# Half of a quad's block moves issued from GpSimd's queue in a fused attention and MLP kernel

## The chip, the cores and the metric

The kernel runs on one core of a Trainium2 chip. A core has five engines with a queue of instructions each: TensorE (PE in the profile), VectorE (DVE), ScalarE (ACT), GpSimd (POOL) and SyncE (SP, which only issues DMAs). Instructions of one engine run in order; between engines, semaphores order them. DMAs are issued from SyncE, ScalarE or GpSimd and are carried out by 16 DMA engines that all of them share. The metric is the device time of one execution in microseconds (us). Before the change it was 395.21 us, the median of two runs (394.13 to 396.29).

## What is computed

Attention with a squared ReLU in place of the softmax, for 8 batches and 12 heads of 448 positions with 64 dimensions, and then a two-layer MLP over all 3584 positions with a PReLU between the layers:

```python
scores = scale * np.matmul(q, k.transpose(0, 1, 3, 2))      # scale = 1/8
attn = np.maximum(scores, 0.0) ** 2 / S                     # S = 448
attn_out = np.matmul(attn, v)
x = attn_out.transpose(0, 2, 1, 3).reshape(B * S, H * D)    # 3584 x 768
h = x @ w_in                                                # 768 x 2048
g = np.maximum(h, 0.0) + alpha * np.minimum(h, 0.0)
out = g @ w_out                                             # 2048 x 768
```

Inputs and output are float32 in HBM. The kernel computes in bfloat16 and accumulates in float32.

## The kernel before

**Quads.** The attention is done in 24 quads, numbered n = 0 to 23: a quad is four heads of one batch, three quads make a batch. A position is written as 7·p + j, with p on 64 partitions and j = 0..6; a *chunk* (n, j) holds the scores of all four heads for the keys of one j.

**From HBM to T.** `load_qk` (L112 to L124) loads a quad's q and k from GpSimd's queue, which casts them to bfloat16 on the way, into the `raw` tiles (three buffers each). The score matmuls contract over the 64 dimensions, so q and k have to lie with the dimension on the partitions: tile `T`, four buffers. For quads 0 to 4, `turn_pe` transposes on TensorE. For quads 5 to 23, `turn_dma` (L194) does it in two steps. DVE transposes each 32x32 block where it lies (L202, one instruction for q and one for k, into a `perm` tile, or into space of `w_mix` that is not yet in use for quads 5, 7 and 8). Then eight plain DMAs (L208) move whole 32-partition stripes between partition groups, SBUF to SBUF, 56 KB each: for each half m (partitions 64m to 64m+63, which hold two of the four heads), for each source stripe a and each destination stripe b. They are issued in the order m, a, b.

**Scores.** `score_mm` (L215) makes a chunk's scores from T in a pair of PSUM banks: for r = 0 it reads partitions 0 to 63 of T, which is the half m = 0, and for r = 1 partitions 64 to 127, the half m = 1. From quad 5 on a chunk is eight matmuls of line L229, four for each r. `relu` (L237 on ScalarE, L239 on DVE) and `square` (L248, L250) follow; `attnv` (L253) multiplies by v once all seven chunks of a quad are there and writes `xT`, the MLP's input.

**MLP.** `f1_mm` (L294) makes one 128-wide block of h in a PSUM bank with six matmuls; `f1_out` takes the negative part on ScalarE (`neg`, L300, two buffers) and joins it on DVE into `gT` (L301). The second layer is L319 for some tiles, and L354 for pairs of tiles that go through a Strassen-like scheme with sums of `gT` (L350) and of the weights (`w_mix`, L332).

**Order of the work.** There is no scheduler. A plan is written out as strings of short words (L525 to L537), and `Walk.step` emits the instructions of a word in that order on all engines. The words that matter here: `cAAD` emits chunks, with the engine of each ReLU; `s0D` a square; `v` an attention-times-v; `f` one block of the first layer; `h`, `e` and `E` parts of one; `d6D` is `turn_dma` of quad 6; `Lq`, `Lv`, `Li` and `Lo` are loads of q and k, v, w_in and w_out. From quad 11 on, a word `n` calls `prepare(n)` (L427), which does `turn_dma(n)`, then loads q and k of quad n + 2 and v of quad n + 1. The first part of the plan around quads 5 to 9 reads (L526, L527, cut):

```python
... m o f s0D f cAAA s0D s1D d5D f f s0D f l5 Lq6 f Lq7 Lq8 g00 Lo1,0,4 s0D cADA s2D vDA cDD ...
B h h cAA h s0D s0D h v d6D l6 Lo1,4 Lv6 h E E E d7D f E f E f f d8D f l8 cAAA s1D f Lq9 f Lv7 ...
```

**Buffers set the waits.** PSUM has eight banks. `take_pair` and `one` (L81, L96) hand out the bank, or pair of banks, that was taken longest ago, so a matmul into a bank waits for whatever still reads it. A load of q waits until the transposes of the quad three before have read its buffer; a load of v (five buffers) until the attention-times-v of five quads before. Each queue also has eight DMA semaphores that it uses in turn, so a DMA waits until the one eight before it on that queue has landed.

**Queues.** Before the change, GpSimd's queue carries only loads (and a few small things at the start), SyncE's the block moves of L208 and the stores of the output (L310).

Of the kernel before, what the change touches and what calls it, by code (L numbers as in the profile page):

```python
# [21 lines left out]
def kernel(  # L22
# [10 lines left out]
    nc = tc.nc  # L33
# [160 lines left out]
    def turn_dma(n, eng="A"):  # L194
        if n in (5, 7, 8):
            w = w_mix[2 + n % 2].rearrange("p k c -> p (k c)")[:, :4 * NJ * D]
            x = w.rearrange("p (i b f c) -> p i b f c", i=2, b=2, c=32)
        else:
            x = perm_pool.tile([128, 2, 2, 2 * NJ, 32], BF16, tag="perm", name="perm")
        for i, name in enumerate("qk"):  # L200
            rows = raw.pop((n, name)).rearrange("p w j d -> p (w j) d")
            nc.vector.transpose(x[:, i].rearrange("p b f c -> p f b c"), rows.rearrange("p f (b c) -> p f b c", b=2))  # L202
        t = T_pool.tile([128, 2, NJ, 128], BF16, tag="T", name="T")
        z = t.rearrange("p i j c -> p i (j c)").rearrange("p i (a f c) -> p i a f c", a=2, c=32)
        for m in range(2):
            for a in range(2):
                for b in range(2):
                    nc.sync.dma_start(out=z[64 * m + 32 * b:64 * m + 32 * b + 32, :, a],  # L208
                                                      in_=x[64 * m + 32 * a:64 * m + 32 * a + 32, :, b])
        T[n] = z  # L210

# [215 lines left out]
    def prepare(n, eng="A"):  # L427
        if n < NQ:
            turn_dma(n, eng)
            land(n)  # L430
        if n + 2 < NQ:
            load_qk(n + 2)
        if n + 1 < NQ:
            load_v(n + 1)
# [4 lines left out]
    class Walk:  # L439
# [12 lines left out]
        def step(self, w):  # L452
# [41 lines left out]
            elif c == "w":  # L494
                i, half = int(rest[0]), int(rest[1])
                weight_mix(i, 4 * half, 4 * half + 4)
            elif c == "g":
                f2(self.b // 2, int(rest[0]), int(rest[1]))
            elif c == "n":
                prepare(self.quad, rest or "A")  # L500
                self.quad += 1
            elif c == "x":
                cast0(int(rest[0]), int(rest[1]), rest[2])
            elif c == "t":
                turn_pe(int(rest[0]), ((rest[1], int(rest[2]), int(rest[3]), rest[4]),))
            elif c == "d":
                turn_dma(int(rest[:-1]), rest[-1])
            elif c == "l":
                land(int(rest))
            elif c == "L":  # L510
                n = [int(x) for x in rest[1:].split(",")]
                {"q": load_qk, "v": load_v, "i": load_w_in, "o": load_w_out}[rest[0]](*n)
            elif c == "i":
                warm(int(rest))
            elif c == "y":
                bank = min(range(8), key=lambda i: (taken[i], i))
                for _ in range(int(rest)):
                    nc.tensor.matmul(psum[:, bank, :128], idle, idle, start=True, stop=True)
            elif c == "z":
                two_queues.append(1)  # L520
            elif c == "b":
                nc.vector.tensor_scalar(beta_sb, alpha_sb, -1.0, 1.0, ALU.mult, ALU.add)
# [48 lines left out]
```

## Time and profile before

| | |
|---|---|
| median of two runs | 395.21 us |
| the profiled execution's own time | 394.87 us |
| its span, first to last instruction | 393.1 us |
| mean granted TensorE clock | 0.991 |
| block moves L208 on SyncE | 152 (128 from `perm`, 24 from `w_mix`), 56 KB each |
| one issue of L208 on SyncE, median | 0.596 us |
| issue to landing of L208, min / median / max | 2.0 / 3.9 / 6.6 us |
| q and k loads of L123 on GpSimd | 76, median issue 0.60 us |
| waits of GpSimd's q loads for DVE's transposes | 129.8 us, 13 times |

The profile is of one execution, and its times count from the first instruction. Busy time is that of compute instructions on an engine; a DMA issue stands in the trace with the time that the queue took to issue it, and its landing is known from the semaphore that it raises. "A <- B" names B as what ended A's wait. In a timeline, a line is start, duration, engine, source line, operation, tiles and count, with the idle time before it in brackets; a line of many matmuls is a run of them. In a table by stages, a line is a stretch of time with the busy time and the count of each engine in it. Matmuls are pipelined, so the pitch from one to the next is the time that counts, not the duration of one.

### The profile page before, as it was taken

How to read it: one execution, taken by the hardware profiler on the slowest of the kernel's cores; microseconds unless marked ns; L12 is line 12 of the kernel's file. 1: busy time of each engine (PE TensorE's matmuls, PEld its weight loads, DVE VectorE, ACT ScalarE, POOL GpSimd, SP SyncE). 2: the span in 40 equal slices, each digit the busy share in tenths (PEclk: the TensorE clock that was granted, in tenths of full speed). 3: DMA queues.
4: the chain of work that ended last, by engine and by line, in shares of the span. 5: the costliest groups of instructions: out<-in, count | busy, mean ns of one | idle time of the engine just before them, and what ended most of it. 6: DMA issues, size and time to landing. Idle time of an engine off the chain costs nothing.

```text
span 393.1 us, 9204 instructions
## 1 busy us (share of the span) xinstructions
PE 372.5 (95%) x3633; PEld 195.9 (50%) x3637; DVE 304.9 (78%) x467; ACT 258.8 (66%) x384; POOL 86.4 (22%) x140
## 2 busy tenths in 40 slices
PE   8899999499989998999989999899999999999996
PEld 6454555144444454545545455445555555555563
DVE  4988988655996989867788886888969875865753
ACT  5987674456766656768668676786587785874400
POOL 8566563500330323011220311303000000000000
PEclk9999999889999999999999999999999999999999
DMA  9999999952677755726766257664333321220024
GB/s 148 191 203 202 207 209 206 223 109 47 100 147 152 117 95 79 166 42 116 136 109 140 43 97 141 108 144 66 76 62 81 76 49 26 64 65 9 2 51 110
DMA packets 51676, 43.38 MB, mean 110 GB/s; under 512 B 8753, under 2 KB 51121, under 8 KB 51633
## 3 DMA queue, kind: packets, MB, share of 16 engines
q0 software_dynamic: 27744, 22.59, 40.0%
q1 hardware_dynamic: 23216, 19.62, 19.6%
q8 instruction: 28, 0.46, 0.5%
q10 hardware_dynamic: 672, 0.59, 0.4%
q14 instruction: 16, 0.12, 0.1%
HBM read 45.62 MB, written 11.01 MB: 144 GB/s over the span
## 4 chain that ended last, share of the span: by engine, by line
PE 72%; DVE 12%; SPq 6%; DMA 4%; issue 3%; ACT 1%; DVEq 0%; ACTq 0%
PE psum L294 30%; PE psum L354 24%; PE psum L260 7%; PE psum L229 6%; SPq L208 5%; DVE perm L202 3%; DVE at L250 3%; DMA T<-perm 2%; PE psum L319 2%; DVE gT L301 2%; DMA T<-w_mix 1%; DVE S L350 1%; PE psum L171 1%; DVE rl L239 1%; PE psum L221 1%
## 5 line engine op out<-in xcount | busy, mean ns | idle before, releaser
L294 PE MATMUL psum<-xT,w_in_sb 128*128 128x448 bf16 x768 | 152.6, 356 | 0.4 <-DVE gT L301 0.4
L237 ACT ACTIVATE rl<-psum 128x896 bf16<-128x896 f32 x128 | 111.4, 929 | 25.9 <-PE psum L229 23.4
L301 DVE SCALAR_TENSOR_TENSOR gT<-neg,beta_sb,psum 128x448 bf16<-128x448 f32 x128 | 84.0, 675 | 36.1 <-ACT neg L300 34.9
L294 PEld LDWEIGHTS <-w_in_sb 128*128 128x128 bf16 x768 | 74.2, 99 | 75.0 <-issue 9.7
L300 ACT ACTIVATE neg<-psum 128x448 f32<-128x448 f32 x128 | 68.9, 546 | 55.3 <-PE psum L294 39.6
L250 DVE TENSOR_TENSOR at<-rl 128x896 bf16<-128x896 bf16 x105 | 62.1, 617 | 3.8 <-ACT rl L237 3.7
L248 ACT ACTIVATE at<-rl 128x896 bf16<-128x896 bf16 x63 | 58.3, 951 | 1.5 <-DVE rl L239 1.2
L123 POOL DMA_DIRECT2D qraw<-in_q_dram x38 | 22.6, 600 | 137.3 <-DVE perm L202 129.8
L354 PEld LDWEIGHTS <-S 128*128 128x128 bf16 x384 | 36.4, 98 | 32.7 <-issue 10.0
L239 DVE TENSOR_SCALAR rl<-psum 128x896 bf16<-128x896 f32 x40 | 43.2, 1086 | 9.3 <-PE psum L229 8.1
L354 PE MATMUL psum<-w_mix,S 128*128 128x384 bf16 x288 | 49.9, 326 | 0.0
L229 PE MATMUL psum<-T 64*32 64x448 bf16 x1064 | 38.0, 358 | 7.1 <-DMA T<-perm 5.4
L354 PEld LDWEIGHTS <-gT 128*128 128x128 bf16 x296 | 28.3, 98 | 20.2 <-issue 1.8
L260 PE MATMUL psum<-at,vraw 64*64 64x448 bf16 x672 | 36.6, 352 | 0.0
L354 PE MATMUL psum<-w_out_sb,gT 128*128 128x384 bf16 x192 | 34.0, 326 | 0.0
L130 POOL DMA_DIRECT2D vraw<-in_v_dram x24 | 17.7, 739 | 51.7 <-PE psum L260 49.7
L229 PEld LDWEIGHTS <-T 64*32 64x32 bf16 x1064 | 12.7, 90 | 29.3 <-issue 26.9
L260 PEld LDWEIGHTS <-vraw 64*64 64x64 bf16 x672 | 19.4, 106 | 14.7 <-issue 6.5
L359 DVE TENSOR_TENSOR osb<-psum,u 128x384 f32<-128x384 f32 (+2 forms) x37 | 19.7, 542 | 9.0 <-PE psum L354 8.4
L123 POOL DMA_DIRECT2D kraw<-in_k_dram x38 | 22.9, 614 | 3.3 <-DMA vraw<-in_v_dram 1.4
L319 PE MATMUL psum<-w_out_sb,gT 128*128 128x256 bf16 (+1 forms) x124 | 22.5, 325 | 0.9 <-DVE gT L301 0.5
L274 DVE TENSOR_SCALAR xT<-psum 128x448 bf16<-128x448 f32 x24 | 14.9, 623 | 10.0 <-PE psum L260 9.9
(46 smaller groups left out, 240.2 us busy)
## 6 DMA issues: line engine op xcount, KB each, us to landing
out_dram<-osb SPq DMA_DIRECT2D x91, 96.0 KB, 2.2
T<-perm SPq DMA_DIRECT2D x128, 56.0 KB, 3.6
vraw<-in_v_dram POOLq DMA_DIRECT2D x24, 224.0 KB, 6.1
qraw<-in_q_dram POOLq DMA_DIRECT2D x38, 112.0 KB, 3.3
kraw<-in_k_dram POOLq DMA_DIRECT2D x38, 112.0 KB, 4.7
w_in_sb<-in_moe_w_in_dram POOLq DMA_DIRECT2D x16, 192.0 KB, 8.2
w_out_sb<-in_moe_w_out_dram POOLq DMA_DIRECT2D x4, 512.0 KB, 10.4
T<-w_mix SPq DMA_DIRECT2D x24, 56.0 KB, 5.3
```

The lines of the kernel that those rows point to most:

```text
L123: nc.gpsimd.dma_start(out=t[64 * m:64 * m + 64].rearrange("p w j d -> p w (j d)"), in_=flat[2 * g + m])
L229: nc.tensor.matmul(ps[lo:lo + 32, r, :S], t[64 * r:64 * r + 64, 1, a, NJ * c + j], moving, start=True, stop=True)
L237: nc.scalar.activation(rl, ps[:, :, :S], ACTF.Relu)
L239: nc.vector.tensor_scalar(rl, ps[:, :, :S], 0.0, None, ALU.max)
L248: nc.scalar.activation(a, rl, ACTF.Square)
L250: nc.vector.tensor_tensor(a, rl, rl, ALU.mult)
L260: nc.tensor.matmul(ps[64 * s:64 * s + 64, r, :S], vv[64 * r:64 * r + 64, s, j, :], a[64 * r:64 * r + 64, s], start=(j == 0), stop=(j == NJ ...
L294: nc.tensor.matmul(ps, w_in_sb[:, km // 2, km % 2, bass.ts(ff, 128)], xT[b][:, km // 2, km % 2, :], start=(km == 0), stop=(km == KM - 1))
L300: nc.scalar.activation(neg, ps, ACTF.Relu, scale=-1.0)
L301: nc.vector.scalar_tensor_tensor(gT[:, ff, (b % 2) * S:(b % 2) * S + S], neg, beta_sb[:, ff:ff + 1], ps, ALU.mult, ALU.add)
L319: nc.tensor.matmul(ps, gT[:, ff, bass.ts(c, 128)], w_out_sb[:, ff, first_col + lo:first_col + hi], start=(ff == 0), stop=(ff == KF - 1))
L354: nc.tensor.matmul(ps, left[:, i], right[:, i], start=(start and i == 0), stop=(i == KH - 1), skip_group_check=not start)
```

## The change

In `turn_dma` the queue of each block move is chosen by its half m: the four of m = 0 go out from SyncE as before, the four of m = 1 from GpSimd. What is moved, and the order m, a, b in which the instructions are emitted, stay. On GpSimd's queue the four stand where `turn_dma` stands in the plan, between the loads that are emitted before and after it; their first one waits for DVE's two transposes. TensorE waits for m = 0 on semaphores of SyncE's DMAs and for m = 1 on semaphores of GpSimd's.

```diff
         for m in range(2):
             for a in range(2):
                 for b in range(2):
-                    nc.sync.dma_start(out=z[64 * m + 32 * b:64 * m + 32 * b + 32, :, a],
+                    (nc.sync, nc.gpsimd)[m].dma_start(out=z[64 * m + 32 * b:64 * m + 32 * b + 32, :, a],
                                                       in_=x[64 * m + 32 * a:64 * m + 32 * a + 32, :, b])
         T[n] = z
```

## The prediction

> **What bounds the kernel now.** I read the page's busy shares and clock row first, then the waits of TensorE, then the timeline of each engine where it waits. TensorE is busy 95% of the span, so a change can give only what TensorE loses to waits and to a lower clock.
>
> ```profile
> PE 372.5 (95%) x3633; PEld 195.9 (50%) x3637; DVE 304.9 (78%) x467; ACT 258.8 (66%) x384; POOL 86.4 (22%) x140
> PEclk9999999889999999999999999999999999999999
> ```
>
> The two eights, about 69 to 88 us, are the only place where the clock falls. The waits of TensorE name the transfers that the change touches:
>
> ```profile
> PE psum L229 <- DMA T<-perm: 5.4, 2, 2.9
> ...
> PE psum L229 <- DMA T<-w_mix: 0.4, 1, 0.4
> ```
>
> Three waits in all, though 19 quads come through these transfers. The chain of waits gives SyncE's issues of L208 5% of the span, but TensorE has gaps for them only here: quad 5 (T read from w_mix, 0.4 us at 53.6) and quad 6. TensorE's timeline around quad 6:
>
> ```profile
> 61.86 8.50 PE L294 MATMUL psum<-xT,w_in_sb 128*128 128x448 bf16 x44
> 73.25 0.37 PE L229 MATMUL psum<-T 64*32 64x448 bf16 x4 [2.90 <-DMA T<-perm]
> 76.12 1.31 PE L229 MATMUL psum<-T 64*32 64x448 bf16 x20 [2.50 <-DMA T<-perm]
> 77.36 9.29 PE L294 MATMUL psum<-xT,w_in_sb 128*128 128x448 bf16 x36
> 86.58 0.76 PE L229 MATMUL psum<-T 64*32 64x448 bf16 x24
> ```
>
> TensorE is free at 70.36. Its first four score matmuls (r=0) need the m=0 half of T, the next four (r=1) the m=1 half: hence two waits. Afterwards 36 matmuls of L294 take 9.29 us; at the pitch of the 44 before (8.50/44 = 0.19 us) they would take 6.95. The stage table shows why (columns: PE, PEld, DVE, ACT and POOL busy, granted clock, DMA share, GB/s):
>
> ```profile
> 70.30:75.20 4.90, 0.43 (x5) 0.13 (x4) 4.63 (x7) 1.70 (x4) 2.49 (x4) 1.00 1.25 227
> 75.20:82.10 6.90, 5.98 (x33) 2.32 (x34) 1.30 (x2) 3.12 (x5) 2.50 (x4) 0.51 1.27 216
> ```
>
> The clock was halved for 6.9 us, in which TensorE worked 5.98: about 2.9 us lost. Waits and clock together: 0.4 + 5.4 + 2.9 = 8.7 us, the most the change can give.
>
> **What is late in quad 6.** Its blocks are transposed by 64.64. SyncE issues eight transfers, six microseconds, and each lands 5.3 to 6.6 us after its issue, because GpSimd's loads keep the DMA engines full:
>
> ```profile
> 64.70 6.00 SPq L208 DMA_DIRECT2D T<-perm  x8
> ```
>
> ```profile
> 53.12 3.04 POOL L145 DMA_DIRECT2D w_out_sb<-in_moe_w_out_dram  x4 [0.23 <-DMA qraw<-in_q_dram]
> 56.14 0.70 POOL L130 DMA_DIRECT2D vraw<-in_v_dram  x1
> 63.95 1.19 POOL L123 DMA_DIRECT2D qraw<-in_q_dram  x2 [7.11 <-DVE perm L202]
> ```
>
> The v load issued at 56.14 landed 13.8 us later: GpSimd's queue is a backlog until about 70.
>
> **The change, step by step.** *Issues.* 19 x 4 = 76 issues leave SyncE (0.596 us median) and 76 go to GpSimd, whose smallest issues (q, k loads, 64 partitions) take 0.60, so each queue needs 2.4 to 2.6 us per quad, side by side, where one needed 5.2 to 6.0. SyncE's stores go out up to 3 us earlier; no engine's waits name a store, so this is worth nothing. GpSimd's busy time grows by 46 us to about 132, far from a bound.
>
> *Order on GpSimd.* The m=1 issues stand in program order: ahead of the loads of q, k (n+2) and v (n+1), and behind earlier ones. They wait for DVE's transposes of quad n, and what is queued behind waits too. Today those q, k loads wait only for a raw buffer (the transposes of quad n-1), so they move later by about a quad. The nearest pair of transposes decides: quad 10's end at 115.40, quad 12's begin at 136.45. The load of 12 would start at 115.4+2.7, issue for 2.4 and land within 5.9 (the longest q, k row after 100 us): 126.4, 10 us early. The other way round, an m=1 issue stands behind a v load that waits for attention-times-v (the longest such wait 16.1 us, ending 288.46); quad 23's transposes end only at 314.80, and the other such waits end 20 us or more before the transposes they would hold up. So nothing on TensorE: 0, at worst a load late, which the 10 us cover.
>
> *Quad 5 (transposed by 44.12).* The four m=1 transfers enter GpSimd's ring behind the v load that lands at 48.83. The 12 q, k loads behind that one land 0.69 to 0.75 us apart (49.69 to 57.95), each with twice the bytes of a T transfer. So m=1 lands by 48.83 + 4 x 0.75 = 51.8 at the latest; TensorE needs it at 53.62. Gain 0.41.
>
> *Quad 6.* Behind quad 5's issues come the loads of quads 6 to 8 (12 x 0.75: landed by 60.8, before their transposes at 62.55, 66.47 and 72.35) and one block of w_out (3.0 more: 63.8). The other three blocks, v(6) and q(9) now stand behind quad 6's own m=1 issues, which wait for DVE until 64.64 - 0.41 = 64.23. So the ring is empty then. m=0: issue 64.3 to 66.8, landing 2.0 (lowest SyncE row) to 5.3 (in the backlog) after the last issue at 66.2. m=1: the wait for DVE costs GpSimd 0.30 today (transpose of q ends 63.65, issue 63.95), so 64.5 to 66.9, the last issue at 66.3; landing after it between 2.6 and 5.9 (rows after 100 us), up to 7.5 in a backlog. I take 2.6 to 3.7, for an empty ring: 68.9 to 70.0. TensorE arrives at 70.36 - 0.41 = 69.95. Both waits go.
>
> *What is late next.* DVE has no gap from 62.01 to 75.01:
>
> ```profile
> 68.49 3.93 DVE L301 SCALAR_TENSOR_TENSOR gT<-neg,beta_sb,psum 128x448 bf16<-128x448 f32 x6
> 72.35 1.10 DVE L202 STREAM_TRANSPOSE w_mix<-qraw 128x896 bf16<-128x896 bf16 x1
> 73.38 1.07 DVE L202 STREAM_TRANSPOSE w_mix<-kraw 128x896 bf16<-128x896 bf16 x1
> 74.37 0.64 DVE L301 SCALAR_TENSOR_TENSOR gT<-neg,beta_sb,psum 128x448 bf16<-128x448 f32 x1
> ```
>
> Walking the plan through take_pair and one: the three score pairs take banks 6-7, 4-5, 0-1, released by gT at 69.73, 71.08 and 71.84; the next f takes bank 2 (72.43), the one after bank 3. Bank 3 is read by the gT at 74.37, behind quad 8's two transposes. All of it moves 0.41 earlier with quad 5. So TensorE does the pairs as banks come free, one f from 72.05 to 73.2, waits 1.45, and starts the second f at 74.66. Five f remain (30 matmuls, 5.75 us): the next scores begin at 80.4, today 86.58. ScalarE's three relu (0.87 each from 72.1) are done by 74.7 and do not bind. **The gain is 86.58 - 80.4 = 6.2 us**, not 8.7: 2.5 of it goes to DVE. It also gives slack: T may land as late as about 72.3.
>
> *After that.* The gaps left on TensorE (0.98 at 110.6, 1.17 at 118.5, three of 1.1 to 1.4) end on DVE, and stay. Quad 7's m=1 stands behind three w_out blocks (2.6 each), a v (1.4) and itself (3.0) from 67.3: 79.5, needed at 90.18 - 6.2 = 84.0. w_out lands by about 75, and weight_mix reads it from 83.2. From quad 9 on, T lands 4.3 us or more before its first matmul already, so faster issue is worth nothing there.
>
> *DVE and GpSimd beside each other.* The q, k issues of 63.95 to 66.33 ran beside DVE's transposes and gT and took 0.59 to 0.62 us, as everywhere (590 to 635 ns); the 41 squares of L250 beside a GpSimd issue have the median of the other 64, 618 ns. I take 0. The Trainium skill, page "SBUF — State Buffer", section "A bandwidth-pool intuition that's wrong (but worth ruling out)", speaks against the change: a GpSimd-issued DMA of 620 ns took 3100 ns beside a DVE copy that holds the shared port. By that rule, as an estimate, four issues of quad 6 would take 12.4 us and T would land near 79, later than now; the rows above do not show it.
>
> *Clock.* TensorE would be busy 2.0 of the 4.7 us from 69.95, 43%. The busy share in the least busy other stretches of that length was 65% at full clock; at 9% the clock fell. I take no fall, and 2.9 us as the other end. The Trainium skill, "TensorE: Matmul & The Clock Gate", Part 1, says the clock halves after an idle window of some 3.4 us; no gap here would be over 1.5, so by the page it stays.
>
> **Rivals.** (1) *DVE does not hold TensorE back*: all 8.7 come, 386.2. Against it: the gapless DVE row. 10%. (2) *The clock falls anyway* in the half-busy stretch: 388.7 + 2.9 = 391.6. 14%. (3) *It doesn't do what it says*: the transfers are late from the full DMA engines, not from their issue, and the ring is not drained; m=1 of quad 6 lands 7.5 after 66.3, at 73.8: second f at 75.8 (+1.15) and the clock falls (+2.9), 392.7. For it: 5.3 to 6.6 us of landing against 2.0 at best. 10%. (4) *Slower*: quad 5's m=1 lands in GpSimd's backlog as late as the v load did, 13.8 us after its last issue at 46.3, at 60.1: TensorE idles 6.5 us at 53.6 and loses the clock, 388.7 + 6.5 + 2.9 = 398.1. It decides from a landing at about 56.9, where 3.3 + 2.9 eat the gain. Against it: loads at that place landed in 8.5 to 8.9. 8%. The rest, 58%, is the forecast.
>
> **Numbers.** The sum stands on the profiled execution, 394.87 us (span 393.1 and 1.8 around it), 0.3 below the median of 395.21: 394.87 - 6.2 = **388.7**. Its own range is 387.9 to 389.9. From (1) to (2), with a little for spread, the range is 386.0 to 392.4; (3) and (4) are left out. About 2%, 7.9 us, is what a measurement of this kernel tells from no change, and the forecast lies inside. Faster by more than that: most of (1) and a tail of the forecast, 0.16. Slower: 0.03. Within: 0.81.
>
> **What would show it.** Right: no wait of L229 on T<-perm at quad 6; a TensorE wait of 1 to 1.5 us on DVE's gT near 74; no 8 in the clock row; GpSimd's L208 x76 at about 0.6 us. Wrong: L208 issues on GpSimd of a microsecond or more, a wait of L229 at quad 5, a wait of L202 on q or k loads, a clock drop near 75.

## The result, and the profile after

The changed kernel takes 389.57 us in the median of two runs (389.12 to 390.03), against 395.21 before: a ratio of 0.9878, with a 95% interval of 0.9847 to 0.9909. Run once more beside experiments it had 388.51 us, 0.9859 (0.9828 to 0.9889), a little under the 389.1 to 390.0 that I expected of it. So it is 1.2 to 1.4% faster, 5.2 to 5.6 us, and within the 2% that the prediction took as the measure of no change. The profiled execution took 389.12 us with a span of 387.1, 6.0 us less than the span before.

The busy shares and the clock row of the changed kernel's page, to be held against those before:

```profile
PE 368.6 (95%) x3633; PEld 194.5 (50%) x3637; DVE 304.9 (79%) x467; ACT 258.7 (67%) x384; POOL 127.7 (33%) x216
...
PEclk9999999999999999999999999999999999999999
```

GpSimd is busy 41 us longer, DVE not at all, TensorE 3.9 us less: its work is the same, but nothing of it ran at half clock. From the waits of TensorE in the changed kernel:

```profile
PE psum L294 <- DVE gT L301: 1.9, 3, 1.3
```

No wait of L229 on a transfer of T is left. What is there instead is DVE. TensorE's timeline around quad 6, changed kernel:

```profile
61.67 8.50 PE L294 MATMUL psum<-xT,w_in_sb 128*128 128x448 bf16 x44
70.09 0.38 PE L229 MATMUL psum<-T 64*32 64x448 bf16 x8
70.94 0.56 PE L229 MATMUL psum<-T 64*32 64x448 bf16 x12 [0.46 <-DVE gT L301]
71.70 0.37 PE L229 MATMUL psum<-T 64*32 64x448 bf16 x4 [0.20 <-DVE gT L301]
72.29 1.30 PE L294 MATMUL psum<-xT,w_in_sb 128*128 128x448 bf16 x6 [0.22 <-DVE gT L301]
74.87 5.83 PE L294 MATMUL psum<-xT,w_in_sb 128*128 128x448 bf16 x30 [1.28 <-DVE gT L301]
80.63 0.76 PE L229 MATMUL psum<-T 64*32 64x448 bf16 x24
```

The first scores of quad 6 start at once, at 70.09. The three pairs of banks and the two f that follow are released one after the other by DVE. The next scores begin at 80.63, before the change at 86.58: 5.95 us, which is the whole difference of the spans. Counted from quad 5's first scores it is more, since they began 0.57 us later in this execution (53.83, before 53.26): 0.8 us came at quad 5, from these scores to the start of the 44 matmuls of L294, and 5.8 at quad 6, from there to the next scores. GpSimd's timeline of the changed kernel shows where its loads went:

```profile
54.85 0.77 POOL L145 DMA_DIRECT2D w_out_sb<-in_moe_w_out_dram  x1 [0.26 <-DMA qraw<-in_q_dram]
65.08 2.16 POOL L208 DMA_DIRECT2D T<-perm  x4 [9.46 <-DVE gT L301]
67.22 2.29 POOL L145 DMA_DIRECT2D w_out_sb<-in_moe_w_out_dram  x3
69.46 0.75 POOL L130 DMA_DIRECT2D vraw<-in_v_dram  x1
70.15 2.22 POOL L208 DMA_DIRECT2D T<-w_mix  x4
```

Three blocks of w_out and a load of v, which before the change were issued at 53.9 to 56.8, now go out after quad 6's transfers, at 67.2 to 70.2. All the instructions of L208 at quad 6, with their landings (changed kernel, 64.4 to 67.3 us):

```profile
L208 SPq DMA_DIRECT2D T<-perm x4: 594/614/645, 64.5 to 66.5; - x4
L208 POOL DMA_DIRECT2D T<-perm x4: 547/548/552, 65.1 to 66.7; - x4
...
DMA to landing us min/median/max: 2.0/2.1/2.3
```

All eight land 2.0 to 2.3 us after their issue, where they took 5.3 to 6.6 before. Two things changed for quad 6 at once, then: half as long an issue, and a wholly different traffic beside it. The experiments take them apart.

### The profile page after: what moved, and what is told of

It is laid out like the page before. It is cut to its first block, busy times and chain, and to the rows that moved or that the text cites. A ratio compares the mean times of both kernels' runs of the same rounds, so it can differ in the third digit from the quotient of the medians.

```text
span 387.1 us, 9270 instructions
## 1 busy us (share of the span) xinstructions
PE 368.6 (95%) x3633; PEld 194.5 (50%) x3637; DVE 304.9 (79%) x467; ACT 258.7 (67%) x384; POOL 127.7 (33%) x216
## 5 line engine op out<-in xcount | busy, mean ns | idle before, releaser
L294 PE MATMUL psum<-xT,w_in_sb 128*128 128x448 bf16 x768 | 150.4, 353 | 1.9 <-DVE gT L301 1.9
L294 PEld LDWEIGHTS <-w_in_sb 128*128 128x128 bf16 x768 | 73.6, 98 | 74.5 <-issue 8.4
L301 DVE SCALAR_TENSOR_TENSOR gT<-neg,beta_sb,psum 128x448 bf16<-128x448 f32 x128 | 84.0, 675 | 33.7 <-ACT neg L300 32.6
L208 POOL DMA_DIRECT2D T<-perm x64 | 34.4, 548 | 157.4 <-PE psum L294 79.7
L250 DVE TENSOR_TENSOR at<-rl 128x896 bf16<-128x896 bf16 x105 | 62.2, 618 | 0.3 <-ACT rl L237 0.2
L229 PE MATMUL psum<-T 64*32 64x448 bf16 x1064 | 37.3, 354 | 1.9 <-DVE rl L239 1.0
L229 PEld LDWEIGHTS <-T 64*32 64x32 bf16 x1064 | 12.4, 89 | 24.2 <-issue 21.6
```

The source lines that it names most:

```text
L208: (nc.sync, nc.gpsimd)[m].dma_start(out=z[64 * m + 32 * b:64 * m + 32 * b + 32, :, a], in_=x[64 * m + 32 * a:64 * m + 32 * a + 32, :, b])
L229: nc.tensor.matmul(ps[lo:lo + 32, r, :S], t[64 * r:64 * r + 64, 1, a, NJ * c + j], moving, start=True, stop=True)
L250: nc.vector.tensor_tensor(a, rl, rl, ALU.mult)
L294: nc.tensor.matmul(ps, w_in_sb[:, km // 2, km % 2, bass.ts(ff, 128)], xT[b][:, km // 2, km % 2, :], start=(km == 0), stop=(km == KM - 1))
L301: nc.vector.scalar_tensor_tensor(gT[:, ff, (b % 2) * S:(b % 2) * S + S], neg, beta_sb[:, ff:ff + 1], ps, ALU.mult, ALU.add)
```

## The experiments

The comparisons are each with the kernel before, run on the same chip in the same set; there were three sets, on three chips. The last two columns are taken from the profiled execution of each kernel. "Quad 5" is the time from quad 5's first scores to the start of the 44 matmuls of L294, "quad 6" from there to the scores behind the next 36 (in the kernel before 53.26, 61.86 and 86.58). Since they count from a point in the work, they are free of what an execution gained or lost earlier.

| kernel | median us | ratio to before, 95% interval | quad 5, us | quad 6, us |
|---|---|---|---|---|
| before | | | 8.60 | 24.72 |
| the change, again | 388.51 | 0.9859 (0.9828 to 0.9889) | 7.83 | 18.97 |
| split at quads 5 and 6 only | 389.64 | 0.9893 (0.9848 to 0.9937) | 7.83 | 20.64 |
| split at quads 7 to 23 only | 389.33 | 0.9881 (0.9850 to 0.9912) | 8.82 | 18.97 |
| all eight on SyncE, one element waits for DVE | 394.47 | 1.0011 (0.9991 to 1.0032) | 8.52 | 24.80 |
| all eight on SyncE, loads held until T lands | 389.33 | 0.9881 (0.9851 to 0.9912) | 8.67 | 18.96 |
| the change, w_out and v ahead of quad 6 | 391.22 | 0.9928 (0.9905 to 0.9951) | 7.83 | 22.11 |
| all eight on GpSimd | 390.27 | 0.9902 (0.9868 to 0.9937) | 7.83 | 18.97 |
| before, TensorE kept busy | 391.74 | 0.9951 (0.9928 to 0.9973) | 8.74 | 21.06 |
| the change, quad 8's transposes later | 386.83 | 0.9823 (0.9781 to 0.9866) | 7.83 | 17.52 |
| before, quad 8's transposes later | 394.15 | 0.9999 (0.9982 to 1.0017) | 8.75 | 23.64 |
| loads held, and quad 8's transposes later | 388.42 | 0.9859 (0.9821 to 0.9896) | 8.71 | 17.52 |

**Which quads give the gain.** First the split at the two quads alone that had shown a wait:

```diff
-                    (nc.sync, nc.gpsimd)[m].dma_start(out=z[...
+                    (nc.sync, nc.gpsimd if n in (5, 6) else nc.sync)[m].dma_start(out=z[...
```

> Only quads 5 and 6 send their m=1 half from GpSimd; quads 7 to 23 send all eight from SyncE as before the change. My theory: TensorE waited for T at these two quads alone, so all of the gain is here: the same time as the changed kernel within 0.5 us (some 389 to 390 us, 5 to 6 us under the kernel before), no wait of L229 on T. Rival, every quad's shorter issue gives a little: two of 19 quads, under 1 us of gain, 394 to 395 us.

389.64 us, the gain of the change within the intervals, and no wait of L229 on T. This agreed with the theory. (Quad 6 took longer than in the change because the clock fell in this execution; the last section comes back to it.) Its complement did not:

```diff
+                    (nc.sync, nc.gpsimd if n > 6 else nc.sync)[m].dma_start(out=z[...
```

> Quads 5 and 6 keep all eight transfers on SyncE; quads 7 to 23 send their m=1 half from GpSimd. My theory: the same time as the kernel before within 0.7 us (0.3 slower to 0.3 faster by the sum: nothing waits for T there). Rival, a share of the gain comes from the many later quads: 1 us faster or more.

It came out at 389.33 us: the gain again within the intervals, with quads 5 and 6 issued by SyncE as before the change. All of it came at quad 6; quad 5's wait stayed. The expectation was wrong, and so was the reading behind it, that a quad's wait goes because that quad's issue is halved. GpSimd's and TensorE's timelines of this kernel (split at quads 7 to 23) show how:

```profile
51.50 2.99 POOL L145 DMA_DIRECT2D w_out_sb<-in_moe_w_out_dram  x4 [0.36 <-DMA qraw<-in_q_dram]
54.46 0.74 POOL L130 DMA_DIRECT2D vraw<-in_v_dram  x1
69.88 2.15 POOL L208 DMA_DIRECT2D T<-w_mix  x4 [14.69 <-PE psum L294]
75.66 2.13 POOL L208 DMA_DIRECT2D T<-w_mix  x4 [3.62 <-DVE gT L301]
77.78 1.22 POOL L123 DMA_DIRECT2D qraw<-in_q_dram  x2
```

```profile
72.47 0.75 PE L229 MATMUL psum<-T 64*32 64x448 bf16 x20 [1.29 <-DVE gT L301]
```

Before the change, GpSimd issued the loads of q, k (9), v (7) and q, k (10) from 63.95 on. Here the m=1 issues of quads 7 and 8 (69.88 and 75.66) stand ahead of them and wait for DVE's transposes, so these loads come at 77.8. The v load issued at 54.46 lands at 68.95 and then nothing competes: quad 6's eight, issued from SyncE at 65.2 to 70.8, land by 72.23 in the landing records. That is 9.85 us after the 44 matmuls began (62.38 here); the limit of about 72.3, up to which the prediction said T may be late for nothing, stands 10.85 after them (61.86 - 0.41 = 61.45 there). What TensorE waits for in the line above is DVE.

**Order or issue time.** All eight stay on SyncE, and a transfer of one element keeps GpSimd's loads back, in two ways. The first waits for DVE's transposes, as the m=1 issues do:

```diff
+        nc.gpsimd.dma_start(out=landed, in_=x[0:1, 1, 1, 2 * NJ - 1, 31:32])
         for m in range(2):
```

> All eight transfers stay on SyncE. In place of the four issues of each quad, GpSimd issues one transfer of a single element that waits for DVE's transposes, so its loads are held back as in the changed kernel. Theory A, the loads' order is what counts: the ring is empty at quad 6, the eight issues take 64.5 to 69.7 and the last lands 2.0 to 2.5 later, at 71.7 to 72.2, where TensorE waits for DVE anyway: 389 to 390.5 us. Theory B, the halved issue time counts: the issue is as long as before, L229 waits 3 us or more for T at quad 6 and the clock falls: 392 to 395 us.

394.47 us, no gain, which would have spoken for theory B. But the trace says otherwise. L208 at quad 6 in this kernel (it stands one line lower):

```profile
L209 SPq DMA_DIRECT2D T<-perm x8: 594/632/925, 64.8 to 69.7; - x8
...
DMA to landing us min/median/max: 2.1/6.1/6.8
```

The first two landed in 2.1 and 2.2 us, the other six in 5.7 to 6.8. The single element let GpSimd go at 65.02, and w_out's blocks started at 65.53, among the eight. The kernel had drained the DMA engines and filled them again too soon; neither theory's premise was met. The second way holds the loads until the last of the eight has landed, at quad 6 alone:

```diff
+        if n == 6:
+            nc.gpsimd.dma_start(out=landed, in_=z[96:97, 1, 1, 2 * NJ - 1, 31:32])
         T[n] = z
```

> The kernel before, all eight transfers from SyncE, and one thing more: at quad 6 alone GpSimd issues a one-element transfer that reads the stripe which the last of the eight writes, so w_out's last three blocks, v(6) and q, k(9) start only when quad 6's T has landed. In the run with a one-element transfer that waited for DVE alone, the first two of the eight landed in 2.1 us and the other six in 5 to 7, because w_out's blocks started at 65.5. Theory A, the loads ahead of or among the transfers are what makes them late: all eight land within 2 to 2.5 us of their issue, the last at 71.7 to 72.2, no clock loss, 388.5 to 390.5 us. Theory B, the halved issue time is what counts: 392 to 394.5 us, L229 waits 2 us or more.

389.33 us, as theory A had it. L208 at quad 6 with the loads held:

```profile
L208 SPq DMA_DIRECT2D T<-perm x8: 594/595/647, 65.1 to 69.7; - x8
...
DMA to landing us min/median/max: 2.0/2.0/2.1
```

Eight issues in a row from one queue take 5.2 us (6.0 before the change, where one of them took 1.4); they land in 2.0 us. TensorE waits for m=1 for 0.8 us, and quad 6 takes 18.96 us all the same, as in the change, since DVE would have held TensorE as long. The gain of the change at quad 6 is had without issuing any transfer from GpSimd. Quad 5, where no loads are held, keeps its wait (8.67 us).

The converse keeps the split and puts the loads back ahead of quad 6:

```diff
-h v d6D l6 Lo1,4 Lv6 h E
+h v Lo1,4 Lv6 d6D l6 h E
```

> The changed kernel, but the last three blocks of w_out and v of quad 6 are issued ahead of quad 6's transfers, not behind them. The issue is halved as in the change; the ring is not drained. Theory A, order of the loads: m=1 of quad 6 lands behind them at 72 to 74, L229 waits 2 to 4 us for T again, 390 us without a fall of the clock and 393 with one. Theory B, issue time: no wait over 0.5 us, 389 to 390 us.

391.22 us, half of the gain. TensorE's timeline of this kernel:

```profile
72.20 1.87 PE L229 MATMUL psum<-T 64*32 64x448 bf16 x24 [2.58 <-DMA T<-perm]
74.00 9.30 PE L294 MATMUL psum<-xT,w_in_sb 128*128 128x448 bf16 x36
```

Issued in 2.8 us from two queues, the eight land 5.2 to 7.4 us later, the last at 72.5 by the landing records. The wait is back, and so is the half clock, from 71.9 for 6.8 us. This is the mechanism of rival (3) (392.7 predicted). What is left of the gain is 0.8 us at quad 5 and 2.6 at quad 6, where T's last transfer lands at 72.5 and not at 75.9. Whether it lands sooner by the shorter issue or because the q, k loads still stand behind is not separated here.

**All eight from GpSimd.**

```diff
+                    nc.gpsimd.dma_start(out=z[...
```

> All eight transfers of every quad from GpSimd, none from SyncE. If T of quad 6 may land as late as 72.3 for nothing, and the loads behind it are what matters, the eight (0.54 us each from 64.8, the last landing near 71.2) cost nothing at quad 6; quad 7's eight stand behind three blocks of w_out and the limit of eight in flight and land at 83 to 84.5, where TensorE needs them from 84.2: 389 to 391 us. Rival, shorter issue is the gain: as slow as the kernel before, 393 to 395 us.

390.27 us. Quad 6's eight issues take 4.29 us and the last lands at 70.19: TensorE waits 0.3 us for it, and goes on to the first f no later than DVE lets it in the change. Quad 7 is late. TensorE's timeline of this kernel:

```profile
85.92 0.37 PE L229 MATMUL psum<-T 64*32 64x448 bf16 x4 [1.79 <-DMA T<-w_mix]
```

Quad 7's eight stand behind w_out's blocks and the limit of eight in flight; the last was issued at 82.91. So GpSimd's queue has a price, at the place where its loads are dense. Quads 5 and 6 take as long as in the change, though no issue is halved.

**The clock by itself.** The kernel before, with 90 matmuls whose results are not used, put ahead of quad 6's first chunks:

```diff
-f f d8D f l8 cAAA s1D
+f f d8D f l8 y90 cAAA s1D
```

> The kernel before, with 90 matmuls on a tile of ones (results not used) ahead of quad 6's first three chunks, so that TensorE is busy from 70.4 to about 75.4 instead of waiting. My theory: the wait for T stays, the clock does not fall at 75.2, and of the 8.7 us in the sum the 2.9 of the clock come: 2.5 to 3.0 us faster than the kernel before (some 391 us). Rival, the half clock cost little because other engines bound that stretch: under 1 us faster.

391.74 us: 2.1 us faster than the kernel before (1.1 to 2.8 by the interval). The fill stands where the wait for T stood: T's last transfer lands at 75.14, the fill ends and the scores begin at 75.73. The half clock is gone, and the 36 matmuls of L294 behind the scores take 6.98 us, not 9.29. The expected 2.5 to 3.0 lies at the upper end of the interval; in this execution the fill outlasted T's landing by 0.6 us, which it may have cost. The stage table of this kernel (columns as in the prediction) has the fill and the stretch that ran at half clock before:

```profile
70.60:75.70 5.10, 5.10 (x91) 5.01 (x89) 4.75 (x7) 1.81 (x4) 1.91 (x3) 1.00 1.24 235
75.70:83.40 7.70, 7.70 (x70) 3.75 (x76) 3.77 (x6) 5.76 (x9) 2.50 (x4) 1.00 1.06 208
```

**What binds after the change.** In the changed kernel, quad 8's transposes were put behind the next first-layer block:

```diff
-f f d8D f l8 cAAA s1D
+f f f d8D l8 cAAA s1D
```

> The changed kernel, with quad 8's two DVE transposes behind the next first-layer block instead of ahead of it. My theory: after the change TensorE waits for the gT that stands behind these transposes (1.28 us at 74.9), so this wait goes and 0.9 to 1.4 us with it: 388 to 388.5 us where the changed kernel has 389.1 to 389.6. Rival, DVE is not what holds the second f: no change.

386.83 us, and all four times (386.77 to 387.05) lie under every time of the changed kernel (388.36 to 390.03). TensorE's timeline with this edit:

```profile
60.92 8.50 PE L294 MATMUL psum<-xT,w_in_sb 128*128 128x448 bf16 x44
...
71.55 6.97 PE L294 MATMUL psum<-xT,w_in_sb 128*128 128x448 bf16 x36 [0.22 <-DVE gT L301]
78.45 0.76 PE L229 MATMUL psum<-T 64*32 64x448 bf16 x24
```

The 36 matmuls run in one piece; the wait of 1.28 is gone, and quad 6 takes 17.52 us, 1.44 less than in the change. The time came out lower than the 388 to 388.5 that I expected, but the times of the change that it was set against were not taken in the same set. This is the fastest of the kernels here. The same edit in the kernel before:

> The kernel before, with quad 8's two DVE transposes behind the next first-layer block instead of ahead of it, the same edit that made the changed kernel 2 to 3 us faster. My theory: in the kernel before TensorE waits for T until 76.1, later than DVE's gT, so it gives nothing: within 0.6 us of the kernel before. Rival, DVE's order costs time in either kernel: 1 us faster or more.

394.15 us, nothing, as expected: there TensorE waits until 75.5, whatever DVE does. Last, the edit on top of the kernel that only holds the loads:

> All eight transfers from SyncE; the loads behind quad 6 held until its T has landed, and quad 8's two DVE transposes behind the next first-layer block. My theory, now that holding the loads gave the whole gain: issuing from GpSimd gives nothing of its own, so this equals the changed kernel with the same edit of quad 8, 386.3 to 387.6 us. Rival: with DVE's wait gone, T's landing (the last at 71.7 instead of 68.9) binds, and some 1 to 2 us are lost against it, 388 to 389 us.

388.42 us. That lies in the rival's range, 1.6 above the split with the same edit, but the two were run on different chips, and beside the kernel before on the same chip their intervals overlap. The trace does not bear out the rival's reason. TensorE's timeline of this kernel:

```profile
62.13 8.50 PE L296 MATMUL psum<-xT,w_in_sb 128*128 128x448 bf16 x44
...
71.84 0.75 PE L231 MATMUL psum<-T 64*32 64x448 bf16 x20 [0.91 <-DMA T<-perm]
...
79.66 0.76 PE L231 MATMUL psum<-T 64*32 64x448 bf16 x24
```

T's last transfer lands at 71.51, and TensorE waits 0.9 us for it. But from the start of the 44 matmuls to the next scores it takes 17.52 us, to the hundredth as long as the split with this edit (60.92 to 78.45 above), where TensorE waits 0.9 us in sum for DVE's gT instead. So at quad 6 the long issue costs nothing in this kernel either. Of the 1.3 us by which the two spans differ (386.2 and 384.9), 0.9 stands at quad 5 (8.71 and 7.83), where this kernel holds no loads.

And at quad 5, too, it is not the halved issue that helps: with all eight from GpSimd, one after the other in 4.7 us, quad 5 takes 7.83 us as with the split, since the q, k loads stand behind all eight; with the one element, which lets these loads start among the eight, it takes 8.52. So none of these kernels shows a gain that needs the issue to be halved; only in the one with w_out and v ahead are the two not separated. A kernel that holds the loads at quad 5 as well was not run.

## Why the prediction was right, and where its steps were not

The time was forecast at 388.7 us, 387.9 to 389.9 as the forecast's own range: 389.57 and 388.51 were measured. By its steps:

- *Only quads 5 and 6 wait for T, and 8.7 us is the most to be had.* Right as to where. Of its three terms, quad 5's 0.41 was too small: the stretch at quad 5 became 0.77 shorter (8.60 to 7.83), and the six profiled executions in which the q, k loads stand behind quad 5's transfers on GpSimd's queue all have 7.83, the others 8.5 to 8.8. The clock's 2.9 was measured as 2.1 (1.1 to 2.8), with a fill that may have cost 0.6 of it.
- *The ring is empty at quad 6, m=1 lands at 68.9 to 70.0.* It landed at 68.69. This step carried the forecast, and its mechanism was right: the prediction names GpSimd's loads as what makes T land late, and works out that w_out, v and q, k now stand behind the m=1 issues. 5.3 to 6.6 us of landing fell to some 2.0 as soon as the loads were gone, with the long issue as with the short one. What it did not say is that this alone is the gain: it lists the halved issue as the first step of the change, and no term of the sum tells the two apart. The belief that a quad gains by its own halved issue was exposed by the split at quads 7 to 23, for which I expected nothing.
- *Rival (3): late from the full DMA engines, not from their issue, and the ring not drained.* Its first half is what the runs show. Its second half did not hold, because the change moves the loads away by its order on GpSimd's queue. With w_out and v put back ahead, it came about: a wait of 2.58 us and the half clock.
- *"What is late next" is DVE; the second f starts at 74.66, the next scores at 80.4.* Measured 74.87 and 80.63, in an execution in which quad 5's scores began 0.57 us later than in the one before. For quad 6 alone the sum had 6.2 - 0.41 = 5.8 us, and 24.72 became 18.96: 5.8. The wait for the gT behind quad 8's transposes was put at 1.45 and was 1.28. Moving these transposes confirmed it.
- *T may land as late as about 72.3 for nothing.* Right as far as it was tried: with the last landing at 72.23 (split at quads 7 to 23) and at 71.65 (loads held) the second f was still released by DVE's gT, after waits of 1.12 and 1.28 us, as in the change, and quad 6 took as long. Counted from the 44 matmuls these landings lie 1.0 and 1.5 us before the limit; the limit itself was not tried.
- *Quad 7's m=1 lands at 79.5, needed at 84.0.* It landed at 82.51, needed at 84.23. The sum took 2.6 us for a w_out block and 1.4 for v; behind one another they landed at 73.27, 76.65 and 79.49, v at 81.34. The margin was 1.7 us, not 4.5, and with all eight on GpSimd it was overdrawn. Mis-sized, without effect on the forecast. Not foreseen was that quad 8's four issues would stretch from 74.94 to 82.16, because a DMA waits for the one eight before it.
- *An issue on GpSimd costs 0.60 us.* 0.547 in the median. *DVE and GpSimd beside each other cost nothing.* DVE's busy time is the same 304.9 us, and the squares of L250 beside a GpSimd issue have a median of 619 ns, the others 618. The slowdown quoted from the page "SBUF — State Buffer" is not seen here: no issue of L208 on GpSimd took over 0.62 us. But the page speaks of a DVE copy, and what ran on DVE beside these issues was mostly L301 and L250, no copy; so the page's own case was not tried.
- *The clock stays.* In the profiled execution, yes. Not always: in the two runs of the result the mean granted clock was 1.000 at 389.12 us and 0.996 at 390.03, so the second probably had a fall (the next section has its like). Rival (2) was no rival but a part of the executions, and that the profiled one was spared is luck.
- *Rivals (1) and (4).* DVE did hold TensorE back, and quad 5's m=1 landed at 50.29, before the 51.8 that was taken as its latest.

## What to carry to other kernels

A transfer that is late has an issue time and a landing time; hold them apart before shortening either. Here the issue looked long (six microseconds in a row) and the landing was what mattered, and the bulk loads that filled the DMA engines were on another queue. When a small transfer that is urgent moves to the queue of the bulk loads, read what its wait holds back: that can be the gain, and it can be had on purpose, by letting the loads wait for it. And follow the stall one step further to what is late next: of 8.7 us 2.5 went to two DVE transposes, which a swap of two words in the plan then gave back in part.

## What the runs showed of the hardware

- At quad 6, with GpSimd's loads in flight, 56 KB from SBUF to SBUF took 5.2 to 7.4 us from issue to landing; with none, 1.8 to 2.4, from SyncE and from GpSimd alike. Loads issued from 0.7 us after the first of eight were enough to make the last six slow.
- The clock of TensorE fell to half in the same place in some executions of a kernel and not in others. With the split at quads 5 and 6 the four times are 388.55, 388.73, 390.55 and 390.68; the mean granted clock is 1.000 in the two faster ones and 0.995 in the two slower ones, and the profile of one of these has the half clock for 3.4 us. The stage table of that execution:

```profile
69.50:74.40 4.90, 2.77 (x32) 1.01 (x31) 4.82 (x8) 4.42 (x8) 3.39 (x6) 1.00 1.19 204
74.40:78.00 3.60, 3.57 (x10) 1.43 (x10) 1.67 (x3) 1.45 (x3) 0.59 (x1) 0.53 1.22 232
```

The profiled execution of the change was as busy in that stretch (2.84 of 5.00 us) and kept the full clock. The longest single gap of TensorE was 1.28 us in both, so a fall does not need an idle window of some 3.4 us, which the table in Part 1 of the Trainium skill's page "TensorE: Matmul & The Clock Gate" gives for the half clock; a stretch that is half idle can do.

What differs between the two is where a grid of time lies. In the clock records of all the traces here, each stretch at one clock, up to the fall at the very end, lasts a whole multiple of 3.413 us (3.41, 6.83, 64.85, 68.27, 382.29), and the first of them begins 3.9 to 7.1 us after the first instruction, differently in each execution; so in these traces the clock changes on a grid 3.413 us wide, whose place differs. In the execution above, the grid's window before the fall, 71.05 to 74.47, was 50% busy. In the profile of the change the grid cut the same stretch so that its least busy window, 72.95 to 76.36, was 62% busy; in the change run again, with the loads held and with the split at quads 7 to 23 it was 55, 56 and 58%. These kept the full clock, while all five falls inside a trace came after windows of 11, 33 or 50%. The half clock lasted until a window that was wholly busy had passed: one window above, two in the kernel before (74%, then 100%). The threshold is not sharp in these records: windows of 48 and 49% elsewhere (all eight on GpSimd from 82.5, the one-element kernel from 68.8) were followed by the full clock. No run set the position of the grid; that it decides is read from these traces. With the edit that closes the gap, the four times lie within 0.3 us, but so they do in the change run again.
